# A fused decode step and its gradients: the order of one DMA queue is searched again, with a rule that puts a store between two loads

## The chip, the cores and the metric

One core of one Trainium2 chip. The metric is the device time of one execution in microseconds. TensorE (PE) multiplies matrices, VectorE (DVE), ScalarE (ACT) and GpSimd (POOL) do the rest, and SyncE (SP) issues DMAs.

## The reference

The forward result of one decode step and all its gradients, in bf16:

```python
xn = layernorm(x)                               # x: 2 x 1 x 576
q  = xn @ wq                                    # 32 heads of 128, 16 key/value heads
p  = softmax(q . k_cache * 128 ** -0.5)         # caches: 2 x 16 x 4096 x 128
A  = (p . v_cache) @ wo
B  = ((xn @ w_gate) * (xn @ w_up)) @ w_down     # 4608 wide
out = x + A + B
```

Returned are `out` (out_0) and the gradients, for a given `grad_out`, of x (out_1), k_cache (out_2), v_cache (out_3), wq (out_4), wo (out_5), w_gate (out_6), w_up (out_7) and w_down (out_8). The batch is 2, so every matrix gradient is a sum of two outer products, yet it is as large as its matrix: the kernel reads 92.48 MB and writes 92.48 MB.

## The kernel before

The work is cut into 16 attention steps (eight groups of two key/value heads, times two batches) and nine pieces of 512 columns of the gated MLP. A step loads two K tiles and two V tiles of 1 MB (128 partitions x 4096 bf16) with `load_kv` (L1152). DVE transposes them in 32 x 32 blocks (L466), PE makes the scores from K and the score gradients from V (both L1277), `softmax` and `dscore` turn these into `pr` and `ds`, PE contracts them with the tiles (L1451), and `head_outer` (L1299) makes the rank-one gradients of V (out_3, from `pr`) and of K (out_2, from `ds`). Each 1 MB of gradient is four PSUM tiles of 128 x 1024, copied to SBUF by ACT (L470) or DVE (L472), and then one store by `put` (L699).

After the two steps of a group, `group_back` makes the gradients of wo (out_5) and wq (out_4). `mlp` makes, from the loads at L1194 (gate and up) and L1207 (down), the products (L877), the gradient of w_down (out_8, L730) and, for several pieces together, those of w_gate and w_up (out_6, out_7). `wide_outer` makes these, and out_4, in 1 MB parts from PSUM tiles of L767; the last piece uses L716. The last 64 rows of out_4, out_6 and out_7 go out as small stores of 64 KB (`tail_outer`, L831). `final_out` and `final_dx` write out_0 and out_1 (L1495).

All tiles of 1 MB come from one pool of 16 buffers called `big`, shared by K/V loads, gate and up loads, transposed tiles and stores; weights have five buffers `ww`.

The order is not written by hand. The kernel is a set of generators (streams); each yields what it wants next: an operation with a cost on an engine, a buffer, an event, a DMA. `Order` runs them against a model of time while the program is built, and what it picks is emitted in that order, engine by engine. At each turn it takes, among all streams, the one that can start first; if that is on an engine, it looks at all streams that could start on the same engine within `SLACK` of it and takes the one of the lowest priority number. SP has a slack of 10000, so on SP the priority alone decides among those that can go on. A priority is `STEP * s + PR[name] + OFF[name][s]`, with `HEAD` or `TAIL` added for the first and last steps; stores have `PR["store"]` on top of their work's priority. `WQ_AT`, `WO_AT` and `MLP_AT` say when the weights' loads and the MLP pieces are due. These numbers come from a search outside the kernel.

SP runs its program in order: an instruction that waits for its buffer or its data holds back every DMA behind it. A DMA also waits, in `Order` and in the program, for the eighth DMA before it. Nearly all transfers go through SP's one queue.

Of the kernel before, what the change touches and what calls it, by code (L numbers as in the profile page):

```python
# [104 lines left out]
class Order:  # L105
# [58 lines left out]
    def start(self, s):  # L164
        r = s.req
# [29 lines left out]
    def run(self):  # L195
        while self.streams:
# [8 lines left out]
            if e is not None:  # L205
                t, _, s, e = min((c for c in cand if c[3] == e and c[0] <= t + SLACK[e]), key=lambda c: (c[1], c[0]))
# [27 lines left out]
            elif r[0] == "dma":  # L234
                self.free[e] = t + r[2]
# [63 lines left out]
OFF = {"turn0": {0: -1015.2, 1: -14.6, 2: -608.5, 3: -352.4, 4: -44.2, 5: -609.4, 6: 1026.5, 7: -575.3, 8: -336.9,  # L299
       9: -48.1, 10: 73.1, 12: 183.6, 13: 1140.9, 15: 354.0}, "turn1": {0: -158.8, 1: 373.8, 2: -399.3, 3: -123.5,  # L300
       4: -561.8, 5: 1792.7, 6: 184.6, 7: -225.4, 8: -1188.5, 9: -525.0, 10: -1211.4, 11: -134.5, 12: 1399.2, 13:
       -786.3, 14: 125.3, 15: -889.4}, "att": {0: -320.6, 1: 25.1, 2: -524.3, 3: 1437.6, 4: -1231.0, 5: 704.1, 6:
       -946.7, 7: -1656.2, 8: -1046.6, 9: 659.5, 10: -617.2, 11: -169.8, 12: 46.5, 13: -31.6, 14: -222.6, 15:
       1033.5}, "dsc": {0: -1811.3, 1: -9.9, 2: 131.1, 3: 301.3, 4: -3.2, 5: 235.2, 6: -975.3, 8: 26.8, 9: 229.2,
       10: -420.4, 11: 210.0, 12: 19.1, 13: 299.2, 14: 9.4}, "conv": {0: -2015.6, 1: 231.3, 2: -0.4, 3: -50.3, 4:
       -1165.8, 5: 1061.5, 6: 135.8, 7: 373.5, 8: -2359.6, 9: 3.5, 10: 1574.4, 11: 172.6, 12: 216.0, 13: 448.3, 14:
       255.6, 15: 10.6}, "con": {0: -32.2, 1: 1152.5, 2: 1696.5, 3: 720.8, 4: 638.1, 5: 104.8, 6: -260.9, 7: -158.3,
# [3 lines left out]
       9: -103.2, 10: -395.3, 11: 2850.9, 12: 125.0, 13: 2376.4, 15: -25.5}, "front": {0: -90.0, 1: 2844.9, 2:  # L311
       -805.5, 3: -966.7, 4: 1527.3, 5: 109.2, 6: 51.9, 7: -924.3, 8: -171.1, 9: -1466.9, 10: -796.2, 11: 95.0, 12:
       407.0, 13: 194.7, 14: 42.9, 15: -116.8}, "back": {0: -1180.5, 1: 591.1, 2: -2708.2, 3: 979.9, 4: 556.1, 5:
# [7 lines left out]
       13: -595.2, 14: -250.1, 15: 5.1}, "mlp": {0: 248.5, 1: 1168.1, 2: -620.3, 3: -398.1, 4: -321.8, 5: 2002.0, 6:  # L321
       162.1, 7: -3.7, 8: -33.1, 9: -2.4, 10: 1014.3, 11: 985.4, 12: 835.4, 13: -9.7, 14: 314.7, 15: -413.5},
       "load": {0: 1074.9, 1: -427.7, 2: 2940.0, 4: -302.0, 5: 501.3, 6: 157.2, 7: 2723.0, 8: 41.7, 9: 175.7, 10:
       -1207.2, 11: -514.7, 12: -5.8, 13: 248.9, 14: 607.8, 15: -253.7}, "wload": {0: -271.1, 1: 208.8, 2: -1828.2,
       3: 108.3, 4: 438.0, 5: -390.0, 6: 623.3, 7: 89.8, 8: -357.2, 9: -50.4, 10: 1806.6, 11: 48.4, 12: -1247.3, 13:
       3030.4, 14: 857.3, 15: 1037.7}, "mload": {0: 867.2, 1: -358.1, 2: -1319.2, 3: 100.2, 5: 58.5, 6: -3446.8, 9:
       -71.5, 10: -371.1, 11: -312.3, 12: 9.2, 13: 247.9, 14: 253.2, 15: -7.2}}
# [6 lines left out]
BIAS = 0.188  # L334
SLACK = {"PE": 0.06, "ACT": 0.25, "DVE": 0.4, "POOL": 10000.0, "SP": 10000.0}
STEP = 28.0
HEAD = {"turn0": -995.0, "turn1": -3790.2, "att": -3348.0, "dsc": 396.0, "conv": -832.5, "con": 1401.5, "out1":
        -1892.2, "out0": 2828.7, "front": 21.6, "back": 291.8, "W0": -1455.9, "W1": -155.0, "BD1": 1364.6, "BD0":
        2903.1, "mlp": 2389.4, "load": -3080.4, "wload": 394.7, "mload": -742.1}
TAIL = {"turn0": 3370.1, "turn1": 9221.8, "att": 665.4, "dsc": 359.0, "conv": 2694.5, "con": 2347.7, "out1": 7925.6,  # L340
        "out0": -1730.3, "front": 756.2, "back": 2986.8, "W0": 3398.4, "W1": -331.2, "BD1": -2581.8, "BD0": -508.7,
        "mlp": -5065.9, "load": 6824.2, "wload": 208.6, "mload": 3569.7}
PR = {"turn0": 1475.9, "turn1": 1614.7, "att": -4652.5, "dsc": -2890.4, "conv": 226.3, "con": -1413.1, "out1":
      3893.4, "out0": 2308.0, "front": 679.0, "back": 881.2, "W0": -1279.8, "W1": -624.6, "BD1": 2069.1, "BD0":
      -1551.4, "mlp": -735.6, "wout": -435.6, "store": -3305.7, "load": -1982.4, "wload": -3953.8, "fin": 5877.7,
      "const": 11595.3, "mload": -2275.6}


def pr(name, s):
# [1252 lines left out]
```

## Time and profile before

| | us |
|---|---|
| three runs: lowest, median, highest | 462.48, 463.48, 464.69 |
| profiled execution: its time | 463.56 |
| profiled execution: its span | 461.7 |
| PE, DVE, ACT, POOL busy | 365.6, 365.9, 337.1, 143.1 |

The span is counted from the first to the last instruction of the profile. "Busy" adds up the time in which an engine executed something. In the table of windows a row gives a stretch of the span, its length, each engine's busy time with the number of instructions, the granted clock of TensorE, the share of time in which the 16 DMA engines were busy, and their rate. In the timeline a row gives start and duration, engine, line and operation. "SPq" is SyncE issuing: its duration is that of the issue, with its waiting in the queue, not of the transfer.

### The profile page before, as it was taken

Reading aid. Unit: us, or ns where it says so; the run is one execution under the profiler, and the core shown is the slowest. Engines: PE = TensorE matmul, PEld = TensorE weight load, DVE = VectorE, ACT = ScalarE, POOL = GpSimd, SP = SyncE. Lnnn points to the kernel's source line nnn. Section 1 sums busy time; section 2 is a strip of 40 time slices with the busy share of each in tenths; the row PEclk is TensorE's granted clock in tenths of the full one; section 3 lists DMA queues with packets and bytes.
Section 4 is the critical chain, followed back from the end, with each engine's and each line's share of the span. In section 5 each row is a group of like instructions: output and inputs, shape, how many; then the busy total and the mean of one; then the engine's idle time right before and its main releaser. Section 6 shows DMA issues by size and latency. Waiting matters only on the chain.

```text
span 461.7 us, 15711 instructions
## 1 busy us (share of the span) xinstructions
PE 365.6 (79%) x6750; PEld 210.9 (46%) x6750; DVE 365.9 (79%) x708; ACT 337.1 (73%) x516; POOL 143.1 (31%) x174
## 2 busy tenths in 40 slices
PE   1687879798987677897687787778988886887986
PEld 1444455556443343454455353544533543443453
DVE  8897888887789687869887688977867887877682
ACT  4268648778986596765857778858857997897873
POOL 0740044303407342560016251140344563053000
PEclk9969575966775677758975798956567685666855
DMA  8999999999999999999999999999999999999985
GB/s 316 414 410 421 412 426 397 416 416 387 357 424 424 407 424 410 422 419 413 411 405 419 418 421 420 424 412 412 409 422 425 415 422 424 422 389 393 423 310 202
DMA packets 40530, 185.97 MB, mean 403 GB/s; under 512 B 3460, under 2 KB 12172, under 8 KB 24076
## 3 DMA queue, kind: packets, MB, share of 16 engines
q1 hardware_dynamic: 40452, 184.96, 98.7%
q8 instruction: 53, 0.87, 0.7%
q14 instruction: 17, 0.14, 0.1%
q10 hardware_dynamic: 8, 0.00, 0.0%
HBM read 92.48 MB, written 92.48 MB: 401 GB/s over the span
## 4 chain that ended last, share of the span: by engine, by line
DMA 48%; PE 24%; DVE 14%; ACT 10%; issue 3%; POOL 1%; SPq 0%; ACTq 0%; DVEq 0%; POOLq 0%
DMA out_dram<-big 23%; DMA big<-in_A_v_cache_dram 15%; ACT big L470 8%; DVE big L466 7%; DMA big<-in_B_w_up_dram 6%; PE ps_o L1299 4%; PE ps_o L730 3%; PE ps_m L1277 3%; DMA big<-in_A_k_cache_dram 3%; PE ps_m L1451 3%; DVE big L472 2%; PE ps_m L895 1%; PE ps_m L681 1%; PE ps_o L767 1%; POOL BD L1265 1%
## 5 line engine op out<-in xcount | busy, mean ns | idle before, releaser
L470 ACT CAST big<-ps_o 128x1024 bf16<-128x1024 f32 (+2 forms) x309 | 278.8, 964 | 47.6 <-PE ps_o L1299 24.1
L466 DVE STREAM_TRANSPOSE big<-big 128x1024 f32<-128x1024 f32 x146 | 176.4, 1223 | 19.5 <-DMA big<-in_A_v_cache_dram 7.5
L1265 POOL TENSOR_TENSOR BD<-vr,mask 128x2048 bf16<-128x2048 bf16 x32 | 115.2, 3602 | 117.8 <-DVE vr L472 47.2
L472 DVE CAST big<-ps_o 128x1024 bf16<-128x1024 f32 (+1 forms) x69 | 73.3, 1064 | 17.4 <-PE ps_o L767 7.8
L1242 POOL COPY W<-rep 32x16 bf16<-32x16 bf16 x128 | 24.6, 192 | 116.5 <-DVE rep L1015 100.5
L1277 PE MATMUL ps_m<-big,W 128*32 128x128 bf16 x2048 | 58.1, 275 | 2.7 <-issue 1.0
L1277 PEld LDWEIGHTS <-W 128*32 128x32 bf16 x2048 | 46.2, 123 | 23.1 <-issue 21.8
L1299 PE MATMUL ps_o<-BD,dd 32*128 32x512 bf16 x256 | 46.6, 502 | 10.0 <-ACT big L470 7.8
L1299 PE MATMUL ps_o<-BD,pp 32*128 32x512 bf16 x256 | 44.5, 472 | 8.8 <-ACT big L470 7.0
L466 DVE STREAM_TRANSPOSE big<-ww 128x1152 f32<-128x1152 f32 (+1 forms) x25 | 33.0, 1319 | 4.1 <-DMA out_dram<-big 4.0
L1451 PE MATMUL ps_m<-big,pp 128*32 128x512 bf16 x256 | 28.9, 540 | 4.4 <-DVE pp L466 3.6
L1451 PE MATMUL ps_m<-big,dd 128*32 128x512 bf16 x256 | 28.5, 539 | 3.4 <-DVE dd L466 2.1
L1299 PEld LDWEIGHTS <-dd 32*128 32x128 bf16 x256 | 11.0, 98 | 26.9 <-issue 19.9
L1299 PEld LDWEIGHTS <-pp 32*128 32x128 bf16 x256 | 10.2, 96 | 28.7 <-issue 24.5
L767 PEld LDWEIGHTS <-xnr 32*128 32x128 bf16 x368 | 13.3, 116 | 14.6 <-issue 13.6
L767 PE MATMUL ps_o<-D,xnr 32*128 32x128 bf16 x256 | 14.0, 269 | 5.5 <-ACT big L470 3.8
L730 PE MATMUL ps_o<-dyr,R 32*32 32x288 bf16 x256 | 17.4, 391 | 1.2 <-ACT big L470 1.2
L1047 POOL COPY qr<-qd 128x256 bf16<-128x256 bf16 x8 | 3.2, 395 | 45.6 <-DVE qd L472 41.8
L730 PE MATMUL ps_o<-dyr,hb 32*32 32x288 bf16 x288 | 14.6, 313 | 2.2 <-ACT big L470 2.1
L1461 ACT ACTIVATE osb<-ps_m 128x512 bf16<-128x512 f32 x14 | 8.5, 604 | 9.9 <-PE ps_m L1451 9.9
L681 PE MATMUL ps_m<-big,wm 128*32 128x128 bf16 x416 | 13.1, 284 | 2.1 <-DVE cr L1403 1.2
L895 PE MATMUL ps_m<-big,Wdy 128*128 128x128 bf16 x162 | 14.0, 254 | 1.0 <-DVE oT L1471 0.6
(210 smaller groups left out, 487.4 us busy)
## 6 DMA issues: line engine op xcount, KB each, us to landing
out_dram<-big SPq DMA_DIRECT2D x74, 1024.0 KB
big<-in_A_k_cache_dram SPq DMA_DIRECT2D x32, 1024.0 KB
big<-in_A_v_cache_dram SPq DMA_DIRECT2D x32, 1024.0 KB
out_dram<-big SPq DMA_DIRECT2D x17, 576.0 KB
ww<-in_B_w_down_dram SPq DMA_DIRECT2D x9, 576.0 KB
ww<-in_A_wo_dram SPq DMA_DIRECT2D x8, 576.0 KB
ww<-in_A_wq_dram SPq DMA_DIRECT2D x8, 512.0 KB
big<-in_B_w_gate_dram SPq DMA_DIRECT2D x4, 1024.0 KB
```

What stands on the lines that cost most here:

```text
L466: nc.vector.transpose(out, in_)
L470: nc.scalar.copy(out, in_)
L472: nc.vector.tensor_copy(out=out, in_=in_)
L681: nc.tensor.matmul(dp[32 * q:32 * q + 32, 0:P], lhsT=W, rhs=view(X, 0, P, xoff(q, s), [[FS, 4], [2, 32]]), start=(s == 0), stop=(s == S - 1))
L730: nc.tensor.matmul(o[32 * q:32 * q + 32, aa, 0:HD2], lhsT=view(t, 32 * q, 32, 2 * A + aa, [[4, 32]]), rhs=dyr[32 * q:32 * q + 32, k * HD2: ...
L767: nc.tensor.matmul(o[:, aa, j * P:(j + 1) * P], lhsT=xnr[32 * a:32 * a + 32, dc * P:(dc + 1) * P], rhs=rhs(a), start=True, stop=True)
L895: nc.tensor.matmul(dh, lhsT=Wdy[:, e, 2 * k:2 * k + P], rhs=view(X[:], 0, P, 64 * k + e, [[D, FC], [2, 32]]), start=(k == 0 and e == 0), s ...
L1242: nc.gpsimd.tensor_copy(view(W_t[t][w][:], 32 * a, 32, 6 + 8 * a, [[G * WW, 4], [WW, G], [1, 2]]), view(rep_t[grp[g]["qs"]][:], 32 * a, 32 ...
L1265: nc.gpsimd.tensor_tensor(BD_t[i][:], view(vr_t[v][:], 0, P, 0, [[0, 16], [1, Dh]]), view(mask16[:], 0, P, 0, [[1, 16], [0, Dh]]), ALU.mult)
L1277: nc.tensor.matmul(sc[32 * cq:32 * cq + 32, :], lhsT=view(W[:], 0, P, (be * G + l) * WW + 6 - 4 * c2 - 2 * l, [[1, 32]]), rhs=view(X[:], 0 ...
L1299: nc.tensor.matmul(o[:, k, :], lhsT=pr2[32 * c4:32 * c4 + 32, :], rhs=BD[32 * c4:32 * c4 + 32, 8 * l + 4 * h2:8 * l + 4 * h2 + 4, :], star ...
L1451: nc.tensor.matmul(ct[32 * j:32 * j + 32, :], lhsT=view(rT, 0, P, 4 * c + 2 * l, [[1, 32]]), rhs=kv_t[kvS[s][t][l]][:, Dh * c:Dh * (c + 4) ...
```

## The change

`Order` gets a rule for SP. Each DMA of the kernel is given a kind: 1 for a large load, 2 for a store of over 500,000 bytes, 0 for the rest. `moved` remembers the last kind that was not 0.

- If the last large DMA was a load and the next candidate is a load, the candidate's start counts as 0.82 us later (`NEAR`).
- If on SP the best candidate is a load that would follow a load, the best store whose priority number is at most 11.1 above it (`APART`) is taken instead, if there is one.

```diff
+        self.moved = None
...
-            return max([s.ready, self.free[r[1]]] + [when(x) for x in lanes[-8:-7]]), r[1]
+            t = max([s.ready, self.free[r[1]]] + [when(x) for x in lanes[-8:-7]])
+            return t + NEAR if r[5] == self.moved == 1 else t, r[1]
...
-                t, _, s, e = min((c for c in cand if c[3] == e and c[0] <= t + SLACK[e]), key=lambda c: (c[1], c[0]))
+                cand = [c for c in cand if c[3] == e and c[0] <= t + SLACK[e]]
+                best = min(cand, key=lambda c: (c[1], c[0]))
+                if e == "SP" and best[2].req[5] == self.moved == 1:
+                    best = min((c for c in cand if c[2].req[5] == 2 and c[1][0] <= best[1][0] + APART),
+                               key=lambda c: (c[1], c[0]), default=best)
+                t, _, s, e = best
...
+                self.moved = r[5] or self.moved
...
-def DMA(engine, cost, nbytes, row=8192):
+def DMA(engine, cost, nbytes, row=8192, kind=0, lanes=16):
...
-    return ("dma", engine, cost, 0.02 + nbytes / 16e3 * packet / row, packet)
+    return ("dma", engine, cost, 0.02 + nbytes / 16e3 * packet / row, packet, kind, lanes)
...
+APART, NEAR = 11.1, 0.82
...
-MLP_AT = [1.14, 5.4, 2.05, 2.45, 26.26, 69.69, 14.36, 0.0, 155.88]
-WQ_AT = [-126, 9, 14, 22, -10, -36, 47, 13]
-WO_AT = [-81, -88, -157, -95, 31, 1, -2, -56]
+MLP_AT = [3.82, 131.28, 5.75, 27.43, 26.49, 131.23, 4.53, 236.98, 110.0]
+WQ_AT = [-268, 8, 14, -32, -521, -139, 39, -50]
+WO_AT = [-67, -128, -467, -183, -162, -298, -288, -105]
...
-BIAS = 0.188
-SLACK = {"PE": 0.06, "ACT": 0.25, "DVE": 0.4, "POOL": 10000.0, "SP": 10000.0}
+BIAS = 0.191
+SLACK = {"PE": 0.02, "ACT": 0.26, "DVE": 0.41, "POOL": 10000.0, "SP": 10000.0}
...
-            yield DMA("SP", 0.36, nbytes, row)
+        for k, (d, x) in enumerate(zip(dst, src)):
+            yield DMA("SP", 0.36, nbytes, row, 2 if nbytes > 500000 else 0, 4 if k in few else 16)
...
-                    yield DMA("SP", 0.36, 1 << 20)
+                    yield DMA("SP", 0.36, 1 << 20, 8192, 1)
```

The loads of wq's main part, wo, w_gate, w_up and w_down get kind 1 in the same way. All of `OFF`, `HEAD`, `TAIL` and `PR` have new numbers, found by a new search with the rule in force. What each generator computes, and with which instructions, stays as it was, except that an eviction may go to the other of ACT and DVE. As the two kernels are built, SP's 229 DMAs have the same sizes in both, and 77 changes between large loads and large stores become 93. All lines after the constants have a number ten higher.

More of the change, by code (lines that the diff above doesn't have):

```diff
@@ L333 @@
 CLK = 2.0
-BIAS = 0.188
-SLACK = {"PE": 0.06, "ACT": 0.25, "DVE": 0.4, "POOL": 10000.0, "SP": 10000.0}
+BIAS = 0.191
+SLACK = {"PE": 0.02, "ACT": 0.26, "DVE": 0.41, "POOL": 10000.0, "SP": 10000.0}
 STEP = 28.0
[L337 to L346, printed above, removed]
+HEAD = {"turn0": 1465.1, "turn1": -6878.4, "att": -800.0, "dsc": -2408.9, "conv": -4840.3, "con": 2704.9, "out1":
+        -1647.2, "out0": 16442.0, "front": 16547.6, "back": -4129.9, "W0": 10929.4, "W1": -4089.4, "BD1": -3335.5,
+        "BD0": 6475.1, "mlp": 6052.0, "load": -2928.8, "wload": -8917.7, "mload": 3814.8}
+TAIL = {"turn0": 12903.2, "turn1": 10231.8, "att": -6933.1, "dsc": -299.9, "conv": 11464.0, "con": 667.5, "out1":
+        12607.2, "out0": -7637.9, "front": -953.8, "back": 1980.1, "W0": 5951.3, "W1": 8819.4, "BD1": -7435.9,
+        "BD0": 1802.2, "mlp": -6560.5, "load": -309.7, "wload": 12678.3, "mload": -12342.8}
+PR = {"turn0": 2330.6, "turn1": 1372.8, "att": -17013.2, "dsc": -7066.8, "conv": -42.4, "con": -1112.1, "out1":
+      6400.4, "out0": 4523.5, "front": 1143.5, "back": 1125.5, "W0": -259.6, "W1": -3608.0, "BD1": 1347.2, "BD0":
+      -2433.2, "mlp": -1210.5, "wout": -3525.8, "store": -8535.9, "load": -2715.0, "wload": -5251.3, "fin":
+      -20776.9, "const": 21594.1, "mload": -7304.0}
 def pr(name, s):
@@ L693, in tail_at, with put @@
         return h, c < FT, c if c < FT else c - FT
-    def put(dst, src, nbytes, row, tag, slot, ready):
+    def put(dst, src, nbytes, row, tag, slot, ready, few=()):
         yield WAIT(*ready)
-        for d, x in zip(dst, src):
-            yield DMA("SP", 0.36, nbytes, row)
+        for k, (d, x) in enumerate(zip(dst, src)):
+            yield DMA("SP", 0.36, nbytes, row, 2 if nbytes > 500000 else 0, 4 if k in few else 16)
             nc.sync.dma_start(d, x)
@@ L823, in tail_outer @@
         dsts = [d.rearrange("(r q) f -> q r f", q=4) if k in few else d for k, d in enumerate(dsts)]
-        yield SPAWN(put(dsts, src, 64 * FS * 2, 1024, "tl", i, done), p + PR["store"])
+        yield SPAWN(put(dsts, src, 64 * FS * 2, 1024, "tl", i, done, few), p + PR["store"])
         def mk(A):
@@ L1172, in load_w @@
                     yield ("lset", Lq[i])
-                yield DMA("SP", 0.4, 128 * 4 * FS * 2, 1024)
+                yield DMA("SP", 0.4, 128 * 4 * FS * 2, 1024, 1)
                 nc.sync.dma_start(ww_t[w][:, 0:4 * FS].rearrange("p (c n) -> p c n", n=FS),
@@ L1177, in load_w @@
             else:
-                yield DMA("SP", 0.36, 128 * GH * D * 2, 4608)
+                yield DMA("SP", 0.36, 128 * GH * D * 2, 4608, 1)
                 nc.sync.dma_start(ww_t[w][:, 0:GH * D].rearrange("p (c n) -> p c n", c=GH),
@@ L1192, in load_w @@
                 sl["G"].append(b)
[L1193 removed]
+                yield DMA("SP", 0.4, 128 * 4 * width * 2, 2 * width, 1)
                 nc.sync.dma_start(G_t[b][:, 0:4 * width].rearrange("p (c n) -> p c n", n=width),
@@ L1205, in load_w @@
                 Ld = Event()
-                yield DMA("SP", 0.36, 128 * FC * D * 2, 4608)
+                yield DMA("SP", 0.36, 128 * FC * D * 2, 4608, 1)
                 nc.sync.dma_start(ww_t[d][:, 0:FC * D].rearrange("p (c n) -> p c n", c=FC),
```

39 lines of the change are left out of this document (19 added, 20 removed), and 21 rows, old and new, of the table OFF.

## The prediction

> **What bounds the kernel now.** I read the page first: the busy shares, the row of DMA shares by slice and the queues.
>
> ```profile
> span 461.7 us, 15711 instructions
> PE 365.6 (79%) x6750; PEld 210.9 (46%) x6750; DVE 365.9 (79%) x708; ACT 337.1 (73%) x516; POOL 143.1 (31%) x174
> ...
> DMA  8999999999999999999999999999999999999985
> ...
> DMA packets 40530, 185.97 MB, mean 403 GB/s; under 512 B 3460, under 2 KB 12172, under 8 KB 24076
> ...
> q1 hardware_dynamic: 40452, 184.96, 98.7%
> ```
>
> One queue, fed by SyncE alone, is 90% busy or more in all slices but the first and the last two. No compute engine is over 79%. So time can come from three places only: a different rate while the queue is busy, stretches where it is not full, and the end, where it is not full at all. I took them in that order from the table of windows.
>
> ```profile
> core 0: us, PE busy (x) PEld busy (x) DVE busy (x) ACT busy (x) POOL busy (x), PEclk, DMA share, GB/s
> 105.00:110.00 5.00, 3.93 (x111) 2.46 (x107) 2.98 (x8) 3.79 (x8) 2.12 (x1) 0.84 1.01 417
> 110.00:120.00 10.00, 9.82 (x173) 5.83 (x169) 7.87 (x14) 9.44 (x13) 5.09 (x2) 0.50 0.95 361
> 120.00:130.00 10.00, 7.87 (x156) 3.80 (x155) 8.64 (x14) 9.77 (x13) 1.53 (x8) 0.84 1.00 371
> 415.00:420.00 5.00, 3.35 (x62) 1.51 (x50) 2.58 (x6) 2.96 (x4) 0.00 (x0) 0.81 0.95 332
> 423.00:437.00 14.00, 13.25 (x214) 6.69 (x205) 10.34 (x20) 12.37 (x19) 0.62 (x1) 0.73 1.01 423
> 270.70:280.40 9.70, 7.86 (x213) 5.21 (x206) 9.70 (x16) 9.10 (x15) 4.14 (x10) 1.00 1.01 422
> 10.00:15.00 5.00, 3.10 (x58) 2.74 (x58) 4.96 (x16) 1.57 (x4) 2.54 (x5) 1.00 1.01 423
> ```
>
> The last two numbers of a row are the DMA share and the rate. From 10 to 15 us only loads have been issued; from 423 to 437 the queue carries a run of stores (SyncE issued nothing else after 415.93, a row further down); from 270.7 to 280.4 it carries (counting packets in order of issue) store, load, store, load. The rates are 423, 423 and 422 GB/s. Loads alone, stores alone and the two in turn cost the same.
>
> Against 417, the row from 105 to 110, the two rows from 110 to 130 lack 10 x (1 - 361/417) = 1.34 us and 10 x (1 - 371/417) = 1.10 us, together 2.4 us, and 415 to 420 lacks 5 x (1 - 332/417) = 1.0 us. In time order, SyncE's own view shows what happened at 110:
>
> ```profile
> start us, us, engine line op out<-in xcount [idle before <-releaser]
> ...
> 102.46 2.54 SPq L1152 DMA_DIRECT2D big<-in_A_k_cache_dram  x2
> 107.64 0.34 SPq L699 DMA_DIRECT2D out_dram<-big  x1
> 108.52 1.14 SPq L699 DMA_DIRECT2D out_dram<-tl  x2
> 112.50 3.26 SPq L699 DMA_DIRECT2D out_dram<-big  x2
> 116.33 2.10 SPq L1152 DMA_DIRECT2D big<-in_A_v_cache_dram  x2
> 119.24 4.55 SPq L699 DMA_DIRECT2D out_dram<-big  x3
> ```
>
> After the two K loads five stores follow, the last two being the first 1 MB pieces of out_6 and out_7, and SyncE stands at each until ACT and DVE have filled its buffer. The next loads, ready or not, wait behind them until 116.33.
>
> The end is read from the chain of waits and two more windows.
>
> ```profile
> 409.17 14.29 DMA big<-in_B_w_up_dram
> ...
> 423.50 0.72 PE ps_m L877 x20
> 424.23 0.52 PE ps_m L1362 x2
> 424.74 0.96 PE ps_o L1299 x6
> 425.71 0.22 PE ps_m L1284
> 425.93 0.11 PE ps_m L1285
> ...
> 458.43 0.41 ACT xy L1491
> ```
>
> ```profile
> 445.00:450.00 5.00, 4.95 (x64) 3.06 (x58) 4.20 (x8) 2.57 (x3) 0.00 (x0) 0.50 0.73 282
> 455.00:460.00 5.00, 2.50 (x18) 1.35 (x18) 1.10 (x5) 1.29 (x2) 0.00 (x0) 0.50 0.42 145
> ```
>
> The last w_up load lands at 423.46, and from there to 458.4 the chain is mostly TensorE work; PE is busy 13.25 of 14 us and 4.95 of 5 us, at a granted clock of 0.73 and 0.50. The last 38 us are bound by compute that starts when that load lands.
>
> **The change part by part.** *The work.* The order as built of both kernels holds the same 229 SyncE transfers with the same 184.95 MB and the same matmuls. Evictions from PSUM move from DVE to ACT only slightly (113 to 107 on DVE, 413 to 419 on ACT, none of 1024 columns). This is worth nothing: neither engine is the bound. The new `lanes` value of a DMA is read nowhere and costs nothing. The priorities, gates, slacks and the bias are nearly all other numbers; they act through the order alone, so I price the places where the order differs and the trace has a price.
>
> *The rule itself.* Among transfers over 0.2 MB, the changes between load and store rise from 77 to 93, and runs of three or more of a kind fall from 28 to 19. By the three rates above the alternation as such is worth 0: 1 GB/s over 9.7 us with three changes is 0.02 us, 0.01 us a change, 0.1 us for sixteen more.
>
> *Fewer gaps behind waiting stores.* In the new order the stretch at 110 us reads: store, two small stores, K load, out_8, out_6, K load, out_7, out_6, wq load, out_7, out_2, two V loads. The wide stores came about one per 3.3 us (3.26 us held the first two, the third left at 119.24), while 1.05 MB takes 2.48 us at 423 GB/s; alone they leave 0.8 us empty each. With a load of 1 MB, then one of 0.5 MB between them, there are 4.96 or 3.7 us of transfers per 3.3 us. I take the full 2.4 us. Only 1.34 of it comes with a DMA share below 1; the 1.10 after it has a share of 1.00 at a low rate, so its packets were slow, and I count it because it follows the gap directly. Bounds: 0 (the gap turns up elsewhere) to -2.4.
>
> *The gap at 415.* The 1 MB out_3 store now stands between the last gate and up loads, and the waiting out_4 store moved ahead of the V loads. DMA share there is 0.95, which is 0.25 us of idleness within the 1.0 us that the rate lacks. I take -0.5; bounds 0 and -1.0.
>
> *Behind w_up.* Everything ahead of the last w_up load is the same but for one out_4 piece of 0.79 MB more: 1.86 us later at 423 GB/s. In the new PE order less stands behind the step that this load releases (L877): 16 fewer L1451 matmuls, 4 fewer L1299, and the L1362 and one L1284/L1285 pair go ahead of it.
>
> ```profile
> 428.52 1.07 PE L1451 MATMUL ps_m<-big,pp 128*32 128x512 bf16 x8
> ```
>
> That is 2 x 1.07 + 4/6 x 0.96 + 0.52 + 0.33 = 3.6 us of PE. If PE is the bound throughout, the end moves by 1.86 - 3.6 = -1.7; if the load alone decides, by +1.9. PE's 13.25 of 14 us is nearer the first; I take half of it, -0.9.
>
> *The very end.* A 1 MB out_3 store now follows the last out_4 store, ahead of the tiny out_1.
>
> ```profile
> L470 ACT CAST big<-ps_o 128x1024 bf16<-128x1024 f32 x255 | 246.0, 1026 | 37.8 <-PE ps_o L1299 24.1 <-DMA out_dram<-big 9.7 <-PE ps_o L767 2.3
> ```
>
> ```profile
> 455.90 0.38 SPq L699 DMA_DIRECT2D out_dram<-big  x1
> 458.87 0.26 SPq L1495 DMA_DIRECT2D out_dram<-xy  x1
> ```
>
> out_4 (0.52 MB, 1.24 us) goes out at 455.90, out_3 one eviction (1.03 us) later, and their 3.7 us of transfers end at 459.6 when out_1 (458.87) could start: +0.7. Bounds 0 and +2.5, the whole transfer.
>
> Sum: -2.4 - 0.5 - 0.9 + 0.7 = -3.1 us. The profiled execution took 463.56 (span 461.7 and 1.9 around it), the median of the three runs is 463.48, so the forecast is 460.4.
>
> **The rivals.** (1) *The queue has the same bytes and the gap comes back elsewhere.* The new order has long store runs too (rows 127 to 133: out_2, out_3, out_5, a small one, out_4, out_2 with one load of 0.6 MB among them), and the 1.86 us by which w_up comes later may eat what PE has less to do. Terms -0.5, +0.7 and about 0: 463.7, no difference.
>
> (2) *A new wait before the last V loads: slower.* In the new order six stores in a row (out_3, out_3, out_5, a small one, and both halves of an out_4 bunch, rows 198 to 203) precede the last two V loads. Before, the second half stood behind them, and SyncE had this:
>
> ```profile
> 403.88 1.87 SPq L1152 DMA_DIRECT2D big<-in_A_v_cache_dram  x2
> ...
> 411.71 3.66 SPq L699 DMA_DIRECT2D out_dram<-big  x1
> ...
> 415.93 21.68 SPq L699 DMA_DIRECT2D out_dram<-big  x9
> ```
>
> If that half leaves as late as then, 411.71 + 3.66 = 415.4, the V loads, gate, out_3 and up (4.2 MB, 9.9 us) follow on an emptied queue, and with out_1's 2.8 us from issue to end w_up lands at 428.1, 4.6 us late. The V data is late too, so PE cannot work ahead. 463.56 - 2.4 + 4.6 + 0.7 = 466.5. It decides from about 411 on (415.4 - 4.6). Against it: in the new PE order all eight L767 blocks of this bunch stand ahead of one more score step than before.
>
> (3) *Alternation does raise the rate.* One stretch ran faster:
>
> ```profile
> 130.00:135.00 5.00, 4.82 (x125) 3.10 (x125) 3.06 (x7) 3.90 (x6) 0.00 (x0) 0.64 1.04 435
> ```
>
> At 435 instead of 423 GB/s, 185.97 MB take 427.5 instead of 439.7 us: 451.3. Against it: loads and stores in turn gave 422. The Trainium skill, "DMA: Bandwidth & Descriptors", section "Two DMAs through the same engine are not ordered", says that an engine's read side and write side are separate queues and that descriptors are pipelined, which would let a load's and a store's halves overlap; by that rule the time would be this rival's, and the 422 row does not agree.
>
> **How the numbers follow.** Half a per cent, 2.3 us, is about what a measurement of this kernel can tell from no change. Forecast (the gap closed, the end no longer): 0.44, 458 to 461.1. Rival 1: 0.28, 461.2 to 465.8. Rival 2, with any other new wait of its kind: 0.26, 465.9 to 469. Rival 3: 0.02. So faster 0.46, same 0.28, slower 0.26. The range: the low end takes all terms at their best, -2.4 - 1.0 - 1.7 + 0 = -5.1, 458.4, and a little more, 457.5; the high end takes in rival 2 at 466.5 and a little more, 467.
>
> **What would show it.** Right: windows from 100 to 130 us all near 417 GB/s with a share of 1; SyncE issuing a load between the out_6 and out_7 stores; the last w_up load landing by about 422 to 424 with PE behind it done earlier. Wrong: a window under 390 GB/s in a new place; the last V loads issued after 411; or L877's start to the end taking longer than the 38 us of now. Rates above 425 in alternating stretches would speak for rival 3.

## The result and the profile after

The changed kernel takes 466.2 us (median of 13 runs, 464.48 to 468.21), the kernel before 464.52 us (13 runs, 462.48 to 465.54). The ratio is 1.0036, with a 95% interval of 1.0023 to 1.005: slower by 1.7 us (1.1 to 2.3). The forecast was 3.1 us faster. The profiled execution of the changed kernel took 466.31 us, its span is 464.5 us, 2.8 us more than before. The profiled execution of the kernel before (463.56) lies 1.0 us under the median of its runs, so the two profiles are further apart than the two medians. The row of DMA shares on the changed kernel's page:

```profile
DMA  8999999999999999999999999999999999999995
```

The bytes and the matmuls are those of before, and one queue is still busy in every slice but the first and the last. The slices hide what matters, as before. The windows show it:

```profile
105.00:110.00 5.00, 4.32 (x68) 2.30 (x71) 4.74 (x7) 4.88 (x9) 0.00 (x0) 0.50 0.93 318
110.00:120.00 10.00, 8.57 (x235) 6.51 (x229) 6.06 (x13) 7.63 (x10) 3.60 (x1) 0.67 0.98 380
120.00:130.00 10.00, 10.00 (x176) 4.06 (x170) 8.45 (x16) 8.57 (x11) 4.17 (x4) 0.57 1.03 413
415.00:420.00 5.00, 4.27 (x43) 1.61 (x31) 3.67 (x9) 3.90 (x8) 0.00 (x0) 0.50 1.01 390
280.00:300.00 20.00, 13.38 (x300) 8.24 (x293) 14.50 (x25) 9.85 (x18) 5.66 (x6) 0.76 1.00 400
300.00:320.00 20.00, 17.95 (x377) 11.28 (x374) 17.85 (x30) 17.06 (x24) 0.00 (x0) 0.59 0.96 368
```

The kernel before has these two rows at 280 and 300:

```profile
280.00:300.00 20.00, 14.62 (x305) 8.78 (x306) 17.53 (x34) 16.60 (x24) 3.44 (x9) 0.91 1.01 420
300.00:320.00 20.00, 15.49 (x327) 10.04 (x324) 14.54 (x24) 13.04 (x21) 5.30 (x2) 0.57 1.02 416
```

Against 417 GB/s the rows from 105 to 130 lack 1.19 + 0.89 + 0.10 = 2.2 us, where before lacked 2.4: the gap that the forecast closed is still there, 5 us earlier. The row at 415 lacks 0.3 instead of 1.0. And there is a new gap: 0.8 + 2.4 = 3.2 us from 280 to 320, where before lacked nothing. Both are more than the chance of one execution: the eight other runs that have this order there show 216 to 352 GB/s from 105 to 110 (the order of before 405 to 417), and x1 and x8, which change nothing near 280 us, have 404 and 402 from 280 to 300 and 331 and 367 from 300 to 320. SyncE's own view of both places in the changed kernel:

```profile
101.21 0.34 SPq L709 DMA_DIRECT2D out_dram<-big  x1
105.47 1.14 SPq L709 DMA_DIRECT2D out_dram<-tl  x2
106.70 0.42 SPq L1162 DMA_DIRECT2D big<-in_A_k_cache_dram  x1
107.91 3.13 SPq L709 DMA_DIRECT2D out_dram<-big  x2
113.16 0.34 SPq L1162 DMA_DIRECT2D big<-in_A_k_cache_dram  x1
```

```profile
269.14 7.62 SPq L709 DMA_DIRECT2D out_dram<-big  x3
...
281.47 0.34 SPq L1217 DMA_DIRECT2D ww<-in_B_w_down_dram  x1
284.31 0.34 SPq L709 DMA_DIRECT2D out_dram<-big  x1
289.54 0.34 SPq L1162 DMA_DIRECT2D big<-in_A_v_cache_dram  x1
289.93 1.08 SPq L709 DMA_DIRECT2D out_dram<-big  x1
292.01 0.34 SPq L1162 DMA_DIRECT2D big<-in_A_v_cache_dram  x1
...
302.96 5.72 SPq L709 DMA_DIRECT2D out_dram<-big  x2
```

At 105 the K load now does stand between wide stores, but SyncE first waits until 105.47 at a small one. From 269 on, three stores, two small ones, w_down and an out_3 store go ahead of the first V load, and another out_3 store between the two V loads. The kernel before issued the same two V loads at 279.50 (the row is in the run at 280 us below). Then SyncE stands until 302.96 and, within the last row, for some 5 us more, at stores that are not ready, and the queue runs dry.

The end is in the chain of waits and in SyncE's last rows:

```profile
408.82 11.75 DMA big<-in_A_v_cache_dram
420.60 1.25 DVE big L476
...
458.85 0.41 ACT xy L1501
```

```profile
456.15 1.48 SPq L709 DMA_DIRECT2D out_dram<-big  x2
459.29 0.26 SPq L1505 DMA_DIRECT2D out_dram<-xy  x1
```

```profile
428.57 0.60 PE L887 MATMUL ps_m<-big,xs 128*32 128x128 bf16 x16
```

The chain now runs through a late V load, not through w_up. The step behind w_up (L887, the old L877) has its second half at 428.57 instead of 423.50, 5.1 us late. From there to the last eviction it is 458.85 - 428.57 = 30.3 us, before 458.43 - 423.50 = 34.9: 4.6 us come back. The windows of these two stretches, first before, then after:

```profile
423.50:458.43 34.93, 32.17 (x510) 17.78 (x509) 23.05 (x49) 26.13 (x37) 0.12 (x1) 0.65 0.88 351
428.57:458.85 30.28, 25.69 (x497) 15.50 (x486) 21.70 (x45) 24.34 (x35) 3.61 (x1) 0.78 0.91 362
```

Two things changed: fewer matmuls are left (497 recorded instead of 510, though the second stretch holds 11 more of L887 itself), and the granted clock is 0.78 instead of 0.65. The runs described below keep one of the two orders in this stretch and show it at several clocks:

| order in this stretch | granted clock | length, us |
|---|---|---|
| of before (before, x4, x14) | 0.65 | 34.8 to 35.1 |
| of before (x11) | 0.70 | 33.6 |
| of before, but for one store (x7) | 0.76 | 32.8 |
| changed, the last store in halves (x13) | 0.66 | 31.9 |
| changed (x6) | 0.71 | 31.6 |
| changed (the changed kernel, x5, x12) | 0.78 | 30.3 |

At a like clock the new order is 2 to 3 us shorter. The rest of the 4.6 us goes with the clock.

The chain of compute so ends only 0.4 us later. But out_1, issued at 459.29, ends the span 5.2 us later, before 2.8: the 1 MB out_3 store stands ahead of it. 0.4 + 2.4 = 2.8 us, the difference of the spans.

### The profile page after: what moved, and what is told of

Its sections match the earlier page's. It is cut to its first block, busy times and chain, and to the rows that moved or that the text cites. A ratio compares the mean times of both kernels' runs of the same rounds, so it can differ in the third digit from the quotient of the medians.

```text
span 464.5 us, 15739 instructions
## 1 busy us (share of the span) xinstructions
PE 379.0 (82%) x6750; PEld 216.4 (47%) x6750; DVE 366.5 (79%) x702; ACT 339.4 (73%) x522; POOL 143.2 (31%) x174
## 4 chain that ended last, share of the span: by engine, by line
PE 35%; DMA 34%; ACT 13%; DVE 11%; issue 4%; POOL 2%; SPq 0%; ACTq 0%; DVEq 0%; POOLq 0%
DMA out_dram<-big 17%; DMA big<-in_A_v_cache_dram 14%; ACT big L480 10%; DVE big L476 6%; PE ps_o L1309 6%; PE ps_m L1287 6%; PE ps_m L1461 5%; PE ps_o L740 4%; DMA big<-in_A_k_cache_dram 3%; PE ps_m L691 2%; PE ps_o L777 2%; PE ps_m L1041 2%; POOL BD L1275 2%; DVE big L482 1%; PE ps_m L905 1%
## 5 line engine op out<-in xcount | busy, mean ns | idle before, releaser
L482 DVE CAST big<-ps_o 128x1024 bf16<-128x1024 f32 (+2 forms) x67 | 72.1, 1077 | 13.0 <-PE ps_o L740 5.1
L1287 PE MATMUL ps_m<-big,W 128*32 128x128 bf16 x2048 | 61.0, 285 | 3.8 <-DVE big L476 1.2
L1287 PEld LDWEIGHTS <-W 128*32 128x32 bf16 x2048 | 47.8, 127 | 21.1 <-issue 19.3
L1309 PE MATMUL ps_o<-BD,pp 32*128 32x512 bf16 x256 | 48.7, 512 | 6.0 <-ACT big L480 4.5
L1461 PE MATMUL ps_m<-big,pp 128*32 128x512 bf16 x256 | 31.6, 591 | 3.0 <-DVE pp L476 3.0
L740 PE MATMUL ps_o<-dyr,hb 32*32 32x288 bf16 x288 | 16.3, 350 | 2.4 <-ACT big L480 1.2
L905 PE MATMUL ps_m<-big,Wdy 128*128 128x128 bf16 x162 | 13.8, 252 | 2.4 <-DVE oT L1481 1.6
L1041 PE MATMUL ps_m<-big,Wdy 128*128 128x128 bf16 x144 | 14.5, 280 | 1.4 <-DVE big L476 1.2
L1362 ACT COPY mr<-m 1x128 f32<-1x128 f32 x16 | 4.7, 295 | 14.9 <-DVE m L1360 14.9
```

Of the source, the lines that this page charges most:

```text
L482: nc.vector.tensor_copy(out=out, in_=in_)
L740: nc.tensor.matmul(o[32 * q:32 * q + 32, aa, 0:HD2], lhsT=view(t, 32 * q, 32, 2 * A + aa, [[4, 32]]), rhs=dyr[32 * q:32 * q + 32, k * HD2: ...
L905: nc.tensor.matmul(dh, lhsT=Wdy[:, e, 2 * k:2 * k + P], rhs=view(X[:], 0, P, 64 * k + e, [[D, FC], [2, 32]]), start=(k == 0 and e == 0), s ...
L1041: nc.tensor.matmul(dp, lhsT=Wdy[:, e, 2 * k:2 * k + P], rhs=view(X[:], 0, P, 64 * k + e, [[D, GH], [2, 32]]), start=(k == 0 and e == 0), s ...
L1287: nc.tensor.matmul(sc[32 * cq:32 * cq + 32, :], lhsT=view(W[:], 0, P, (be * G + l) * WW + 6 - 4 * c2 - 2 * l, [[1, 32]]), rhs=view(X[:], 0 ...
L1309: nc.tensor.matmul(o[:, k, :], lhsT=pr2[32 * c4:32 * c4 + 32, :], rhs=BD[32 * c4:32 * c4 + 32, 8 * l + 4 * h2:8 * l + 4 * h2 + 4, :], star ...
```

## The experiments

The theories, by the letters of the expectations. **A**: the last 1 MB store sets the end. **B**: what the queue loses in the middle counts in full. **C**: a gap that is closed comes back elsewhere. **D**: the compute-bound end absorbs the middle. **E**: loads put behind stores cost the time. (In x2, B stands for room at the end, as is said there.) In all but the copies and the run without the rule, the order found by the planner is written down instruction by instruction and repeated, with only the moves that are named. The "loss" of a stretch is its length less what its packets take at their usual durations (309, 159, 84 and 46 ns for 8192, 4096, 2048 and 1024 bytes, sixteen at a time). Ratios are to the kernel before; times in us are worked out from them with 464 us.

**The end.** Four runs.

```diff
 kernel before, SyncE (x7)
-out_2_dram<-big2 128x4096
 out_0_dram<-xy
 out_5_dram<-big3 128x2304
 out_4_dram<-tl0 4x16x512
 out_4_dram<-big1 128x4x512
+out_2_dram<-big2 128x4096
 out_1_dram<-xy
```

> The kernel before with one row of SyncE's order moved and nothing else: the last out_2 store, ready at about 449 us, is issued behind the last out_4 store, ahead of out_1. Theory A (1 MB last in the queue sets the end): out_1 is issued at 458.9 as before, but its transfer stands behind 1 MB issued at 456.5, and the span ends 5 instead of 2.8 us after out_1's issue: 2.2 to 2.5 us more, ratio 1.005. If the queue is empty enough at the end to send 1 MB beside the last 2.4 us of compute, the cost is the 0.7 us of my prediction or less, ratio 1.000 to 1.0015.

```profile
456.62 1.85 SPq L699 DMA_DIRECT2D out_dram<-big  x2
458.83 0.26 SPq L1495 DMA_DIRECT2D out_dram<-xy  x1
```

out_1 is issued when it was before (458.87), and the span of 463.8 ends 5.0 us later instead of 2.8. So one profiled execution shows A's 2.1 us. Twelve timed runs show less: ratio 1.0017 (1.0000 to 1.0035), 0.8 us, 0 to 1.6. That is my own +0.7; A's full price is not borne out by the times. The trace of x7 shows one thing more. Its order is that of before up to the moved store, yet the last w_up load goes out at 411.57 instead of 409.17, and the last eviction still comes at 458.39 instead of 458.43. So two executions of one order can lie 2.4 us apart at w_up; here the stretch behind it, at a granted clock of 0.76 instead of 0.65, made up for it.

```diff
 kernel before (x2): as above, and the L1299 block that completes this store
-PE L1299 block, its ACT eviction (ahead of L1089)
+PE L1299 block, its ACT eviction (behind the last L716, ahead of L1539)
```

> The kernel before with the opposite move: the last L1299 block of its last out_2 store, the eviction and the 1 MB store go behind the last out_4 store, ahead of out_1, as in the changed kernel. All else keeps its order. Theory A: the end is 2.4 us later (out_1 at 5.2 instead of 2.8 us before the span's end), 466.9 us, ratio 1.005. Theory B: the end has room for 1 MB, and the time stays within 0.5 us of the kernel before, ratio 1.000. My prediction's own term for this was +0.7 us, ratio 1.0015.

Ratio 1.006 (1.0036 to 1.0084), 2.8 us. The sum fits A, but for another reason:

```profile
456.47 0.61 PE L1299 MATMUL ps_o<-BD,dd 32*128 32x512 bf16 x2 [1.10 <-ACT big L470]
```

The moved block waits 1.10 us for an eviction on ScalarE and holds up the last chain behind it: L1549 comes at 458.48 instead of 456.23. The run does not tell A from the rest.

```diff
 changed kernel (x1)
+PE L1309 block, its ACT eviction, out_3_dram<-big1 (ahead of the second-last out_2 store)
-PE L1309 block, its ACT eviction, out_3_dram<-big1 (ahead of out_1)
```

> The changed kernel with one block of work moved: the last L1309 block, its eviction and the 1 MB out_3 store that it completes go ahead of the second-last out_2 store, so that the second out_4 half and then out_1 end the program, as in the kernel before. All else keeps its order. Theory A (the last store sets the end): out_1 was issued at 459.29 and landed with the span's end 5.2 us later; without 1 MB ahead of it, it lands 2.8 us after its issue, as in the kernel before: 2.4 us less, 463.8 us, ratio to the kernel before 0.998. The moved block may delay the last chain by its own 0.6 to 1 us of TensorE, which would leave 1.4 of the 2.4. Theory B (the end only mirrors what was lost in the middle of the run, at 290 to 325 us): no change, 466.2 us, ratio 1.0036.

Ratio 1.0052 (1.0032 to 1.0072): no gain. The span (465.0) now ends 2.8 us after out_1's issue, as A says, but out_1 is issued at 462.21 instead of 459.29. The block stands ahead of the last chain, in a stretch where ScalarE is busy without a pause (5.00 of 5 us from 440 to 445). At the end it cost a transfer; here, it seems, it costs compute. The trace does not settle how much: from the step behind w_up on, the granted clock was 0.71, in the changed kernel 0.78.

```diff
 changed kernel (x8)
+out_3_dram<-big1 128x2048 (first half, ahead of the last out_2 store)
-out_3_dram<-big1 128x4096 (ahead of out_1)
+out_3_dram<-big1 128x2048 (second half)
```

> The changed kernel with its last 1 MB out_3 store cut in two: the half that is ready by 442 us goes ahead of the last out_2 store, the other half (0.52 MB) stays where the whole was. No compute moves. Theory A: the last transfer is 1.24 us shorter at 423 GB/s, so 1.2 us less, 465.0 us, ratio 1.001. Theory C: no change, ratio 1.0036.

Ratio 1.0047 (1.003 to 1.0064), no gain; from out_1's issue to the end it is still 464.4 - 459.96 = 4.4 us. By x7's times the last store costs about 0.8 us (0 to 1.6), and no edit of the changed kernel got it back.

**A load put into the gap at 112 us.**

```diff
 kernel before, SyncE (x4)
 out_6_dram<-big12 128x2x2048
+ww1<-in_A_wq_dram 128x4x512
 out_7_dram<-big9 128x2x2048
 ...
-ww1<-in_A_wq_dram 128x4x512
 ww2<-in_A_wo_dram 128x2304
```

> The kernel before with one load moved: the first 0.52 MB wq piece of the second group, issued at 143.86 us, goes between the out_6 and out_7 stores at 112.8 us, where the queue was short of work. All else keeps its order. My prediction's step (a load between the waiting stores fills the gap, and what is filled is gained): 0.52 MB at 423 GB/s is 1.24 us, so 1.2 us less, 463.3 us, ratio 0.997. Theory C (a gap closed comes back elsewhere): the rows from 110 to 120 rise by 0.52 MB, a later row loses it, and the time stays within 0.4 us, ratio 1.000. If the buffer of that piece is not yet free at 112.8, SyncE stands there and the time rises.

```profile
110.00:120.00 10.00, 8.94 (x176) 5.14 (x166) 7.84 (x13) 8.99 (x12) 4.77 (x2) 0.61 1.00 364
120.00:130.00 10.00, 9.13 (x170) 4.24 (x159) 6.88 (x12) 8.60 (x11) 2.15 (x9) 0.50 1.01 408
```

The two rows have 364 and 408 GB/s instead of 361 and 371: they lack 1.3 + 0.2 = 1.5 us instead of 2.4. The ratio is 1.0006 (0.9988 to 1.0024); the 0.997 that my step gives lies outside. The load took 0.9 us off the gap, and by the interval the time fell by at most 0.6 us. The 120 to 130 row is clear of chance (351 to 371 GB/s in the runs that keep the order of before there); where the time went instead, no row shows.

**The waits at 290 us.** Three runs of the changed kernel, with the buffers of the V loads exchanged for others, from that place on.

```diff
 x3, buffer of: first V load, later K load
-big4, big1
+big1, big4
 x5, x6, buffer of: first V load, X transpose, later X transpose
-big4, big1, big13
+big1, big13, big4
 x6 also, SyncE
+big3<-in_A_v_cache_dram
 out_3_dram<-big9
-big3<-in_A_v_cache_dram
```

> The changed kernel with two buffers exchanged from one place on: the V load that stood at SyncE from 284.65 to 289.54 us for its buffer (an out_2 store was still leaving it) goes into the buffer of the K load that comes four rows later, and that one into its. No order changes. Theory B (what was lost at 290 to 325 us sets the time): the V load is issued up to 4.9 us earlier, DVE and the stores behind it follow, most of the 4.0 us that the five rows from 290 to 325 lack against 417 GB/s is saved, and the time falls by 2 to 4 us, to 462 to 464, ratio 0.994 to 0.999. Theory C (a gap closed comes back elsewhere): the rows from 290 to 325 are nearer 417, other rows lose as much, and the time stays within 0.7 us of 466.2, ratio 1.002 to 1.005.

> The changed kernel with three buffers exchanged in a ring from one place on, so that neither the V load (that waited until 289.54 us) nor the transposes on VectorE beside it (which waited in its place until 288.9 us when two buffers were exchanged) needs the buffer that the out_2 store is leaving; a later transpose gets it. No order changes. Theory B (the gap at 290 to 325 us sets the time): the second V load goes out by 289 to 290 instead of 292.0, the loss between 280 and 320 us falls from 3.3 to under 2 us, and the time falls by 1.5 to 3 us, ratio 0.997 to 1.001. Theory C (a gap closed comes back elsewhere): the time stays within 0.7 us of the changed kernel, ratio 1.002 to 1.006.

> The same three buffers, and the second V load goes ahead of the out_3 store that the new order puts between the two V loads of a step (the change's own rule, undone at this one place). Theory B with the rule at fault here: a store takes 2.48 us of the queue, so the second V load goes out 2.5 us earlier than with the buffers alone, the loss between 280 and 320 us falls by 2 us more, ratio 0.993 to 0.998. Theory C: within 0.7 us of the changed kernel, ratio 1.002 to 1.006.

The rates from 280 to 300 and 300 to 320 us and the ratios:

| kernel | GB/s | GB/s | ratio (interval) |
|---|---|---|---|
| changed | 400 | 368 | 1.0036 (1.0023 to 1.005) |
| x3 | 419 | 332 | 1.0059 (1.0034 to 1.0083) |
| x5 | 422 | 350 | 1.0044 (1.0027 to 1.006) |
| x6 | 421 | 358 | 1.0041 (1.0023 to 1.006) |

The first row of each gets well, and no time is gained: C. The second row is lower than the changed kernel's, but x1, with the changed kernel's order here, has 331 as well, so this alone does not show that the gap moved. Taken together the two rows lack 2.6 to 4.0 us against 417 GB/s in x3, x5 and x6, and 3.1 to 4.7 in the changed kernel, x1 and x8. In x3 the wait went from SyncE to the transposes on VectorE: both wanted the buffer of one out_2 store, which takes 20 us to leave.

```profile
269.31 19.59 DMA out_dram<-big
...
288.99 2.38 DVE big L476 x2
...
291.44 14.98 DMA big<-in_A_v_cache_dram
```

In x6 the V loads go out at 288.07 and 290.5 or so, 1.5 us earlier than in the changed kernel; in x3 and x5 the first goes out 3.0 and 2.1 us earlier (286.53 and 287.43), the second within 0.6 us of where it was. So these runs took a wait away, but left the loads far behind the 279.50 of the kernel before.

**Loads behind stores.** Here the kernel before gets one feature of the new order, at the same place.

```diff
 kernel before, SyncE (x11)
-big2<-in_A_v_cache_dram 128x4096
-big10<-in_A_v_cache_dram 128x4096
 out_2_dram<-big12 128x4096
 out_3_dram<-big0 128x4096
+big2<-in_A_v_cache_dram 128x4096
+big10<-in_A_v_cache_dram 128x4096
```

> The kernel before with one move in SyncE's order: the two V loads issued at 279.5 us go behind the out_2 and the out_3 store that followed them, as the changed kernel has it at this place. Nothing else moves. If the gap at 300 to 325 us of the changed kernel comes from this, a loss of 2 to 4 us appears between 280 and 320 us, where the kernel before loses 0.1. Theory B: the time rises by as much, ratio 1.005 to 1.009. Theory D: the loss appears and the time stays within 1 us, ratio 0.999 to 1.002. If no loss appears, the gap of the changed kernel has another cause.

SyncE in the kernel before, then in x11, then x11's two windows:

```profile
277.02 0.34 SPq L699 DMA_DIRECT2D out_dram<-big  x1
279.50 2.97 SPq L1152 DMA_DIRECT2D big<-in_A_v_cache_dram  x2
284.57 4.21 SPq L699 DMA_DIRECT2D out_dram<-big  x3
```

```profile
279.04 6.50 SPq L699 DMA_DIRECT2D out_dram<-big  x3
286.49 1.76 SPq L1152 DMA_DIRECT2D big<-in_A_v_cache_dram  x2
```

```profile
280.00:300.00 20.00, 12.53 (x258) 7.04 (x257) 12.57 (x23) 13.46 (x17) 1.53 (x8) 0.80 1.02 422
300.00:320.00 20.00, 17.57 (x328) 11.34 (x332) 18.02 (x30) 15.55 (x26) 7.20 (x2) 0.60 0.98 369
```

This is the clearest of the runs. The V loads are 7 us later. VectorE, which transposes what they bring, has 12.57 instead of 17.53 busy us from 280 to 300, the stores that depend on it are late, and from 300 to 320 the queue has 369 instead of 416 GB/s: 20 x (1 - 369/416) = 2.3 us lost. The ratio is 1.0042 (1.0026 to 1.0057), 2.0 us (1.2 to 2.6). Two loads put behind two stores, out of 229 transfers, make the kernel before as slow as the changed one, and here the loss in the middle is nearly all in the time, against D. In the trace w_up goes out at 412.39 instead of 409.17, but x7 had 411.57 without this move, so the timed runs carry this and not the one trace. out_1 goes out at 460.23 instead of 458.87, and the span ends 4.3 instead of 2.8 us after that.

The gap is like that of the changed kernel in size (369 and 368 GB/s), not in shape: in rows of 2.5 us x11 is lowest from 315 to 320 (298 and 275 GB/s), the changed kernel from 307.5 to 312.5 (262 and 305), and it has a first dip from 290 to 295 (362 and 323) that x11 lacks.

```diff
 kernel before, SyncE (x14)
-big15<-in_A_v_cache_dram 128x4096
-big3<-in_A_v_cache_dram 128x4096
 out_3_dram<-big5 128x4096
 out_3_dram<-big8 128x4096
+big15<-in_A_v_cache_dram 128x4096
+big3<-in_A_v_cache_dram 128x4096
```

> The kernel before with the same kind of move at another place: the two V loads issued at 357.78 us go behind the two out_3 stores that followed them (359.22 us on). Nothing else moves. If loads put behind two stores always cost what they cost at 280 us, a loss of 2 to 3 us appears between 360 and 400 us (where the kernel before loses 0.15) and the time rises by about 2 us, ratio 1.003 to 1.006. If only places where the stores behind wait on those very loads are hurt, the loss stays under 1 us and the ratio is 0.999 to 1.002.

The kernel before, then x14:

```profile
360.00:380.00 20.00, 17.33 (x324) 10.02 (x320) 17.27 (x32) 18.59 (x29) 10.83 (x16) 0.77 1.01 420
380.00:400.00 20.00, 14.82 (x213) 7.18 (x208) 14.50 (x26) 15.34 (x25) 4.88 (x6) 0.65 1.01 424
```

```profile
360.00:380.00 20.00, 13.06 (x228) 7.05 (x225) 12.87 (x24) 13.53 (x20) 7.30 (x10) 0.70 1.00 397
380.00:400.00 20.00, 17.42 (x231) 7.60 (x230) 14.82 (x26) 16.11 (x26) 9.08 (x11) 0.62 0.95 364
```

A gap again, 80 us later: 20 x (1 - 397/420) + 20 x (1 - 364/424) = 3.9 us of queue lost. The ratio is 1.0019 (1.0006 to 1.0033), 0.9 us (0.3 to 1.5): slower, though by far less than the queue lost. Both expectations miss: the loss is larger than either said, and the time is that of the smaller one. So the price of a lost stretch is not fixed: 2.0 of 2.3 us in x11, 0.9 of 3.9 here. What absorbs the rest in x14 no run shows.

```diff
 changed kernel, SyncE (x12)
+big12<-in_A_v_cache_dram
+big9<-in_A_v_cache_dram
 ww1<-in_B_w_down_dram
-out_3_dram<-big12
-big4<-in_A_v_cache_dram
-out_3_dram<-big9
-big3<-in_A_v_cache_dram
+out_3_dram<-big4
+out_3_dram<-big3
```

> The changed kernel with its order mended at one place: the two V loads issued at 289.54 and 292.01 us go ahead of the w_down load and of the two out_3 stores (issued at 281.47, 284.31 and 289.93 us) that stood before them, into the two buffers that those stores used, and the two stores with their eight blocks of compute come after, in the loads' old buffers. Everything else keeps its order. Theory E (loads put behind stores at this place cost the changed kernel what the opposite edit cost the kernel before): the loss between 280 and 320 us falls from 3.3 to about 1 us and the time by about 2 us, 464.2 us, ratio 0.999 to 1.000. Theory C (what is closed comes back): within 0.7 us of the changed kernel, ratio 1.002 to 1.006. If the moved compute now waits for its buffers and holds up TensorE and ScalarE behind it, the time rises.

> The edit with the two V loads first, and the last 1 MB out_3 store cut in two halves as well. Theory E and the half store's worth add up to 2 to 3 us: 463.2 to 464.2 us, ratio 0.997 to 1.000, which would be no slower than the kernel before. Theory C: ratio 1.002 to 1.006.

x13 joins the edits of x12 and x8. The two windows of x12:

```profile
280.00:300.00 20.00, 11.09 (x233) 6.02 (x233) 11.27 (x17) 7.92 (x12) 4.32 (x5) 0.59 0.98 396
300.00:320.00 20.00, 18.32 (x301) 11.21 (x301) 16.77 (x30) 15.31 (x25) 0.00 (x0) 0.50 0.75 280
```

Both miss: 1.0099 (1.0072 to 1.0126) and 1.0075 (1.0055 to 1.0094). In x12 the V loads do go out 8 to 9 us earlier (from 280.78 on), but into the two buffers that the stores had used. The stores' eight blocks of compute ran from 285 to 293 us instead of from 279 to 285 (in x12 TensorE has 11.09 busy us from 280 to 300, in the changed kernel 13.38), and the gap came later and deeper. These two orders do not mend the place. That the late V loads cause the gap in the changed kernel too is thus argued from x11, where the opposite edit makes a gap of that size, and not shown in that kernel itself.

**More and fewer bytes.**

```diff
 x9, kernel before, the stores of 284.57 us:  nc.sync.dma_start(d, x)
+                nc.sync.dma_start(d, x)
 x10, changed kernel, two out_3 stores
+                d, x = d[:, 0:256], x[:, 0:256]
             nc.sync.dma_start(d, x)
```

> The kernel before with two stores issued twice (the out_2 and out_3 stores that SyncE issues from 284.57 us on): 2.1 MB more in the queue and no other work. At 423 GB/s that is 5.0 us of transfers. Theory B (the queue is the bound, its time in the middle counts in full): 468.5 us, ratio 1.011. Theory D (the last 40 us are bound by compute, and what the queue loses in the middle is largely absorbed): under 1.5 us more, ratio 1.000 to 1.003.

> The changed kernel with two out_3 stores (issued at 284.31 and 289.93 us) cut to 256 of 4096 columns, so that most of these two blocks of out_3 is not written; all compute stays. The queue carries 2.0 MB or 4.6 us less, just ahead of the two V loads that came late. Theory B: 461.6 us, ratio 0.994 or lower. Theory D: the V loads land up to 4.6 us earlier and the loss between 280 and 320 us shrinks, but the time falls by under 1.5 us, ratio 1.000 to 1.004.

x9 took 1.0225 (1.0198 to 1.0253) and says nothing on B: the second copy of a store waits for the first to land in the same place, so SyncE stood from 286 to 298.89 and from 299.7 to 307.41 us. x10 has 0.9981 (0.9962 to 1.0), against 1.0036 about 2.6 us less, for 4.6 us fewer transfers: between B and D. D's reason does not hold, for in the trace the V loads go out at 289.41 and 291.98 us, as in the changed kernel, and do not get earlier. (This profiled execution, 466.03 us, was the slowest of the twelve, whose median is 462.71.)

**The rule and the alternation.**

```diff
 changed kernel (e1)
-APART, NEAR = 11.1, 0.82
+APART, NEAR = -1e9, 0.0
```

> The changed kernel with its rule for SyncE switched off (no store is preferred between two loads, no delay of a second load), all its numbers kept. They were fitted with the rule, so the order changes in many places and 81 instead of 93 changes between load and store are left. If the rule itself saves time, this is slower than the changed kernel by more than 1 us, ratio over 1.006; by my prediction's term alternation is worth 0, and what the other order does by accident decides: between 0.995 and 1.015, no sign expected.

1.0162 (1.013 to 1.0195). All the other numbers were searched together with the rule, and the order without it differs in many places; this prices a spoiled order, not the rule.

```diff
 copy of 64 tiles, run of loads, then run of stores: 4 for K, 1 for V (m1)
-    for (src, dst), run in zip(tiles, (4, 1)):
+    for (src, dst), run in zip(tiles, (1, 4)):
 (m2)
```

> A copy alone, nothing of the reference's computation: the 32 K tiles of 1 MB to out_2 in runs of four loads and four stores, then the 32 V tiles to out_3 as load, store, load, store, eight tiles ahead, through the same queue and 16 buffers. The other outputs are not written. If the change's alternation is worth 0, as my prediction has it, both halves run at the same 420 to 424 GB/s within 0.5%. If loads and stores in turn overlap (rival 3), the second half is 3% faster, 435 GB/s; if the direction change costs something, it is slower.

> The copy alone again, nothing of the reference's computation, with the two patterns exchanged: K to out_2 as load, store in turn, V to out_3 in runs of four. In the first copy the runs of four went at 423 GB/s and the turns at 428. If alternation makes that 1%, the first half now has 428 and the second 423; if it is the place in the run or the tensors, the first half has 423 and the second 428 again.

The first fence is m1 (runs of four, then in turn), the second m2 (in turn, then runs), one execution of each; the last number is GB/s.

```profile
40.00:140.00 100.00, 0.00 (x0) 1.00 1.01 423
190.00:290.00 100.00, 0.00 (x0) 1.00 1.01 428
```

```profile
40.00:140.00 100.00, 0.00 (x0) 1.00 1.01 427
190.00:290.00 100.00, 0.00 (x0) 1.00 1.01 426
```

In turn 427 and 428, in runs 423 and 426: 4 GB/s more for K, 2 for V, 0.7% on average. Between a kernel of runs of four alone and one of strict alternation that would be 3 us of 440; sixteen more changes among some 200 large transfers are a few tenths, by this estimate. The Trainium skill, "DMA: Bandwidth & Descriptors", section "Two DMAs through the same engine are not ordered", has the read side and the write side of an engine as separate queues with descriptors pipelined; the sign of the copies agrees, and its size here is 0.7%.

## Why the prediction was wrong

- **The rule itself, 0**: right but for tenths (m1, m2).
- **Fewer gaps behind waiting stores, -2.4**: this step failed. It took one stretch of the new order, saw a load between the wide stores, and credited the whole lack of the stretch. The lack stayed: 2.2 us instead of 2.4, so 0.2 was gained where 2.4 was credited, because SyncE now stands at a smaller store ahead of that load until 105.47. And x4 shows that even a load that does go into the gap, and takes 0.9 us off it, saves at most 0.6 us. The step had the bound 0 and the rival "comes back elsewhere" beside it, and took the other end.
- What the part-by-part pricing left out: it priced the places where the trace of before showed a gap, and never asked where the new order puts **loads behind stores**. At 280 us it does so with two V loads, and the queue lacks 3.2 us from there to 320. x11 prices the same move in the kernel before at 2.0 us (1.2 to 2.6), as much as the whole change (1.7). One of the prediction's own signs of being wrong, a window under 390 GB/s in a new place, was this one.
- **The gap at 415, -0.5**: right in the trace, the row lacks 0.3 instead of 1.0.
- **Behind w_up, -0.9**: with 1.86 us of transfers more ahead of it and 2.9 us of gaps closed, the load was to be 1.0 us earlier; its step came 5.1 us later. Of the 3.6 us of TensorE work that no longer stands behind it I credited half, 1.8; the traces show 2 to 3 us at a like clock. The rest of the 4.6 us is a higher granted clock, which I had not foreseen: luck, in the trace's favour. The net is +0.4.
- **The very end, +0.7**: 2.4 in the profiled execution; by the times of x7 0.8 (0 to 1.6). The size was about right, and one profile overstated it.
- **Rival 1** (463.7) had the right mechanism at 105 us and no eye for the new gap. **Rival 2** named a new wait before the last V loads, decisive from about 411: they went out from 408.82, and the chain of waits does run through one of them. But the queue was late long before: by 400 us it had moved about 2 MB less than that of before, 5 us of transfers, and 1.4 MB of this from 280 to 320. That the rival's 466.5 is near the measured 466.2 is luck. **Rival 3**: excluded as a gain of 3%; no 40 us stretch of the changed kernel is above 420 GB/s, and the copies show 0.7%.

Together x11's 2.0 and x7's 0.8 are more than the 1.7 of the change, and the shorter tail of compute works against them, by 2 to 3 us in the traces. No run adds these up, and the other places where the two orders differ were not tried one by one, so the sum stays open. Open is also why the gap at 300 us stays when the V loads of the changed kernel are 1.5 us earlier (x6), and how much earlier they would have to be.

## What to carry to other kernels

In a kernel bound by one in-order queue, read a new order for what it delays, not only for what it fills: a load that goes behind two 1 MB stores goes out later by more than their own 5 us (7 in x11, 5.9 in x14), and the stores that need its data can leave a hole 20 to 30 us further on. A gap in the trace is not yet a price: it cost 2.0 of 2.3 us in x11, 0.9 of 3.9 in x14, and to fill 0.9 us of one in x4 gained nothing measurable. So try it with one moved row before crediting it. Before a shorter stretch of compute is put down to less work, compare the granted clock of the two traces. And a wait for a buffer that is taken away often only changes its owner: first see whether the load gets earlier.

## What the runs showed of the hardware

- A 1 MB transfer takes 2.48 us of the queue, yet in the copies a store lands 19.7 us after its issue (m1's median): with eight transfers outstanding a buffer is held for about eight times 2.48 us. In x3 SyncE issues at 281.60, 284.04, 286.53, 288.96 and 291.44, one transfer apart, although the loads and stores are of several kinds: it waits for the eighth before. (At the last of these a transpose, too, ends just before, at 291.37.)
- The span ends 5.2 and 5.0 us after the last 2 KB store is issued when 1 MB was issued shortly ahead of it (the changed kernel, x7), and 2.8 us after it without (before, x1).
- With one order of the last 35 us, the stretch took 34.9 us at a granted clock of 0.65, 33.6 at 0.70 and 32.8 at 0.76 (before, x11, x7).
- There is a small difference in rate between loads and stores in turn (427.5 GB/s) and in runs of four (424.5), in one execution of each copy.
